# Centring of w_out ranked later on VectorE, and one more square of chunk 0 on ScalarE

## The chip, the cores and the metric

The kernel runs on one core of a Trainium2 chip. A core has five engines with instruction streams of their own: TensorE (PE) multiplies matrices, VectorE (DVE) and ScalarE (ACT) do elementwise work, GpSimd (POOL) does elementwise work on SBUF and issues the loads here, and SyncE (SP) issues stores and transposing transfers. All transfers run on the core's 16 DMA engines. The metric is the device time of one execution in microseconds (us); a profile's span is the part of it from the first to the last recorded instruction.

## What is computed

Linear attention without a mask, a norm over each head, and then an expert layer with a SoLU activation and a layer norm:

```python
# q, k, v: (8, 8, 576, 64); g_norm: (64,)
kv  = einsum('bhsd,bhse->bhde', k, v)
o   = einsum('bhsd,bhde->bhse', q, kv)
x   = o / sqrt(mean(o * o, -1) + 1e-6) * g_norm      # -> (4608, 512)
# w_in: (512, 1024); w_out: (1024, 512); g_ln: (1024,)
h   = x @ w_in
e   = exp(h - max(h)); u = h * e / sum(e)
ln  = (u - mean(u)) / sqrt(var(u) + 1e-6) * g_ln
out = ln @ w_out
```

The kernel does not divide by sum(e): it keeps u = h * exp(h) and takes the scale out of the layer norm at the end. For each token it needs the mean of u, of u squared and of e.

The subtraction of the mean is moved into the weights. w_out is multiplied by g_ln row by row, and the mean of the result over the 1024 rows is subtracted from each row. This is the centring. out is then u times the centred w_out, scaled by one number for each token.

## The kernel before

The tokens are worked through in nine chunks of 512: chunk c below 8 holds 512 of the 576 tokens of batch c, and chunk 8 holds the last 64 of every batch. A chunk goes through these pieces, which the source names as they are named here:

- `k`, `v`, `q`: loads on GpSimd (lines 212 and 220), for batches 0 and 1 in two halves. The buffers of each hold three batches.
- `kv_mm` (L286) and `kv` (L304, L306): the products of k and v, and their copies to SBUF, some of them on VectorE and some on ScalarE.
- `qT_mm` (L314) and `qT` (L321, L323): transposes of q on TensorE and their copies. From batch 4 on a transposing DMA on SyncE does this.
- `o_mm` (L348), `sq` (L363), `s_mm` (L369), `ln`, `ex` (L373, L377), `x` (L390): attention output, its square, the mean over a head, one over the root, and x.
- `h_mm` (L471), `exp` (L479), `u` (L486): eight blocks f = 0 to 7 of 128 columns of h, each 512 tokens wide.
- `usq` (L495 on ScalarE, L497 on GpSimd): the square of each block of u. `es` (L503, GpSimd): the sum of two neighbouring blocks of e.
- `sums` (L537): 80 narrow matmuls that sum u, usq and es over the columns. `turn` (L545) and `stats` (L553 to L558) on VectorE and `rstd` (L562, L564) on ScalarE make the scale of each token from them.
- `out` (L585): for each of four groups of 128 tokens two halves of four matmuls of u with the centred w_out. The first half uses blocks 0 to 3, the second blocks 4 to 7. `ob` (L617, VectorE) multiplies by the scale and `store` (L626, SyncE) writes 256 KB.

Once in the kernel, `w_mean` (L570) computes the mean over the rows of w_out into a PSUM bank, and eight pieces `w_center` (L576, VectorE) write the centred w_out in bf16, one for each block f. The first half of every `out` needs `w_center` 0 to 3, the second half 4 to 7.

The order on each engine is fixed when the program is built. Every piece is added to a plan with its engine, an assumed length, a rank, and the pieces that it needs. The planner then takes, again and again, the ready piece that can start first by its own reckoning, and the lower rank where several can start at the same time. PSUM banks and SBUF buffers enter through the fields `uses` and `first`: two banks each for h, out and o, one each for s and misc. The lists that come out are final: on the chip each engine works through its own and waits at each instruction for what it needs.

In chunk 0 the `usq` rank is fixed at -0.6 for all blocks, and `sums` has rank -0.4. Blocks 2, 4, 6 and 7 of `usq` are on ScalarE and the other four on GpSimd. The centring has ranks 0.05 to 0.89, and `u` of block 7 of chunk 0 has rank 0.875 + 0.04 = 0.915.

Of the kernel before, what the change touches and what calls it, by code (L numbers as in the profile page):

```python
# [84 lines left out]
def kernel(  # L85
# [27 lines left out]
    NC = B + 1  # L113
# [19 lines left out]
    plan = Plan({**banks, **bufs})  # L133
# [113 lines left out]
    for b in range(B):  # L247
        at = b - 9.0 if b > 1 else (-2.0, -1.5)[b]
        behind = [] if b < 2 else [("h_mm", 0, 0)] if b == 2 else ([("gate", b - 1)] if b - 1 in XBAR else []) + [("h_mm", b - 3, 2 if b == 3 else 0)]
        for g, hs in enumerate(heads(b)):  # L250
            part = 0.1 * g
            n = len(heads(b))
            for i, (name, src) in enumerate((("k", k), ("v", v))):
                plan.add((name, b, g), "pool", 0.75 if n == 1 else 0.6, at + part + 0.01 * i,
                         lambda name=name, src=src, b=b, hs=hs: load_kv(name, src, b, hs),
                         behind, uses=[(name, b)] if g else [],
# [3 lines left out]
                     uses=[("q", b)] if g else [], first=[] if g else [("q", b)], load=2.7 / n if b < 4 else 3.3)  # L260
# [11 lines left out]
    def kv_tag(b, x):  # L272
        return "s" if b > 1 and x else "misc"
# [123 lines left out]
    for c in range(NC):  # L397
# [4 lines left out]
        if c < B:  # L402
            for xs in ((0,), (1,)) if c < 2 else ((0, 1),):
# [3 lines left out]
                         uses=[("k", c), ("v", c)], first=[(kv_tag(c, x), "kv", c, x) for x in xs])  # L407
                for x in xs:
                    for part in range(3):
                        plan.add(("kv", c, x, part), kv_engine(c, x), 0.25, rg + 0.05,  # L410
                                 lambda c=c, x=x, part=part: kv_copy(c, x, part), [("kv_mm", c, g)],
                                 uses=[(kv_tag(c, x), "kv", c, x)])
        if c in XBAR:
            plan.add(("qT", c), "sp", 1.8, r - 0.1, lambda c=c: q_turn(c),
                     [("q", c, 0)] if c < B else [("q_last", b) for b in range(B)],
                     uses=[("q", c)] if c < B else [], first=[("qT", c)])
# [3 lines left out]
        for hf in range(2):  # L420
            g = group(c, hf)
            tag = ("out", "h")[c] if c < 2 and hf else "o"
            if c not in XBAR:
# [11 lines left out]
                     uses=[("qT", c)], first=[(tag, c, hf, z) for z in range(2)])  # L435
            for z in range(2):
                i = (c, hf, z)
                rz = r + w * (0.4 + 0.5 * hf + 0.12 * z)
                if (c, hf) in COPIED and z:
                    plan.add(("oc", i), "dve", 0.62, rz, lambda i=i: o_copy(*i), [("o_mm", c, hf)],  # L440
                             uses=[(tag, *i)], first=[("oc", i)])
                    plan.add(("sq", i), "pool", 1.05, rz + 0.01, lambda i=i: o_sq_copy(*i), [("oc", i)],
                             uses=[("oc", i)], first=[("osq", i)])
                else:
                    plan.add(("sq", i), "act", 0.57, rz, lambda i=i: o_sq(*i), [("o_mm", c, hf)],
                             uses=[(tag, *i)], first=[("osq", i)])
                stag = "h" if i in ((0, 0, 1), (0, 1, 0)) else "s"
                plan.add(("s_mm", i), "pe", 0.22, rz + 0.02, lambda i=i, stag=stag: s_mm(i, stag), [("sq", i)],
                         uses=[("osq", i)], first=[(stag, i)])
                if c == 0:  # L450
                    plan.add(("ex", i), "act", 0.6, rz + 0.04, lambda i=i: s_rsqrt(*i), [("s_mm", i)],
                             uses=[(stag, i)], first=[("rst", i)])
                else:
                    plan.add(("ln", i), "act", 0.6, rz + 0.03, lambda i=i: s_ln(*i), [("s_mm", i), "table"],
                             uses=[(stag, i)], first=[("lss", i)])
                    plan.add(("ex", i), "act", 0.6, rz + 0.04, lambda i=i: s_exp(*i), [("ln", i)],
                             uses=[("lss", i)], first=[("rst", i)])
                plan.add(("x", i), "dve", 0.67, rz + 0.06, lambda i=i: x_mul(*i),
                         [("ex", i)] + ([("x", (c, 0, 0))] if (hf, z) != (0, 0) else []),
                         uses=[(tag, *i), ("rst", i)] + ([("x", c)] if (hf, z) != (0, 0) else []),  # L460
# [3 lines left out]
    def h_bank(c, f):  # L464

        return ("h", "h", "o", "o", "out", "h", "h", "h")[f] if c == 0 else "h"

    def h_mm(c, f):
        t = T["h", c, f] = bank((h_bank(c, f),), [128, 512], FP32)
        for dt in range(NP):  # L470
            nc.tensor.matmul(  # L471
                t[:, :], w_in_sb[:, dt, f * 128:(f + 1) * 128], T["x", c][:, dt].rearrange("p a b c -> p (a b c)"),
                start=(dt == 0), stop=(dt == NP - 1),
            )

    def h_exp(c, f):
        if f % 2 == 0:
            T["e", c, f // 2] = tile_of(("e", c, f // 2), [128, 2, 512], FP32)
        nc.scalar.activation(  # L479
            out=T["e", c, f // 2][:, f % 2, :], in_=T["h", c, f][:, :], func=AF.Exp, bias=zero_t[:, :]  # L480
        )

    def h_u(c, f):
        if f == 0:
            T["u", c] = tile_of(("u", c), [128, NF, 512], BF16)
        nc.vector.tensor_tensor(  # L486
            out=T["u", c][:, f, :], in0=T["h", c, f][:, :], in1=T["e", c, f // 2][:, f % 2, :], op=MUL
        )

    def u_sq(c, f, engine):  # L490
        if f == 0:
            T["usq", c] = tile_of(("usq", c), [128, NF, 512], BF16)
        dst, src = T["usq", c][:, f, :], T["u", c][:, f, :]
        if engine == "act":
            nc.scalar.activation(out=dst, in_=src, func=AF.Square, bias=zero_t[:, :])  # L495
        else:
            nc.gpsimd.tensor_tensor(out=dst, in0=src, in1=src, op=MUL)  # L497

    def e_sum(c, n):
        if n == 0:  # L500
            T["es", c] = tile_of(("es", c), [128, NF // 2, 512], BF16)
        e = T["e", c, n]
        nc.gpsimd.tensor_tensor(out=T["es", c][:, n, :], in0=e[:, 0, :], in1=e[:, 1, :], op=ADD)  # L503

    xs = [(hf, z) for hf in range(2) for z in range(2)]
    for c in range(NC):
        for f in range(NF):
            r = c + f / 8
            plan.add(("h_mm", c, f), "pe", 0.87, r, lambda c=c, f=f: h_mm(c, f),
                     [("w_in", f // 4), *[("x", (c, *i)) for i in xs]], uses=[("x", c)], first=[(h_bank(c, f), "h", c, f)])  # L510
            plan.add(("exp", c, f), "act", 0.57, r + 0.02, lambda c=c, f=f: h_exp(c, f),
                     [("h_mm", c, f), "table"] + ([("exp", c, f - 1)] if f % 2 else []), uses=[(h_bank(c, f), "h", c, f)] + ([("e", c, f // 2)] if f % 2 else []),
                     first=[] if f % 2 else [("e", c, f // 2)])
            plan.add(("u", c, f), "dve", 0.62, r + 0.04, lambda c=c, f=f: h_u(c, f),
                     [("exp", c, f)] + ([("u", c, 0)] if f else []), uses=[(h_bank(c, f), "h", c, f), ("e", c, f // 2)] + ([("u", c)] if f else []),
                     first=[] if f else [("u", c)])
            engine = "act" if f in {0: (2, 4, 6, 7), 1: (), NC - 1: (1, 3, 5, 6, 7)}.get(c, (2, 6)) else "pool"
            plan.add(("usq", c, f), engine, 0.57 if engine == "act" else 1.05, r + 0.15 if c else -0.6,
                     lambda c=c, f=f, engine=engine: u_sq(c, f, engine), [("u", c, f)] + ([("usq", c, 0)] if f else []),
                     uses=[("u", c)] + ([("usq", c)] if f else []), first=[] if f else [("usq", c)])  # L520
            if f % 2:
                n = f // 2
                plan.add(("es", c, n), "pool", 1.28, r + 0.1, lambda c=c, n=n: e_sum(c, n),
                         [("exp", c, f)] + ([("es", c, 0)] if n else []), uses=[("e", c, n)] + ([("es", c)] if n else []),
                         first=[] if n else [("es", c)])
# [49 lines left out]
    def w_center(f):  # L575
        nc.vector.scalar_tensor_tensor(  # L576
            out=w_out_sb[:, f, :], in0=w_out_f[:, f, :].bitcast(FP32), scalar=g_ln_sb[:, f:f + 1],
            in1=T["mean"][:, :], op0=MUL, op1=SUB,
        )
# [48 lines left out]
    plan.add("w_mean", "pe", 2.0, -0.5, lambda: [w_mean(f) for f in range(NF)], ["w_out", "g_mean", ("o_mm", 0, 1)],  # L628
             first=[("out", "mean")])
    for f in range(NF):  # L630
        plan.add(("w_center", f), "dve", 0.67, 0.05 + 0.12 * f, lambda f=f: w_center(f), ["w_mean"], uses=[("out", "mean")])
    for c in range(NC):
        r, rs = (c + 1, c + 1) if c else (0.55, -0.5)
        parts = [[("u", c, f) for f in range(NF)], [("usq", c, f) for f in range(NF)], [("es", c, n) for n in range(NF // 2)]]
# [1 line left out]
                 uses=[("u", c), ("usq", c), ("es", c)], first=[("misc" if c else "h", "sum", c)])  # L636
        plan.add(("turn", c), "dve", 0.25, rs + 0.14, lambda c=c: sums_turn(c), [("sums", c)],
                 uses=[("misc" if c else "h", "sum", c)])
        plan.add(("stats", c), "dve", 0.65, rs + 0.16, lambda c=c: stats(c), [("turn", c)], uses=[("misc" if c else "h", "sum", c)])
        plan.add(("rstd", c), "act", 0.45, rs + 0.17, lambda c=c: rstd(c), [("stats", c)])  # L640
        for x in range(2 if c == NC - 1 else 0):
            engine = ("dve", "act")[x]
# [3 lines left out]
                     uses=[("h", "acc", x)] + ([("ob", c, 3)] if x else []), first=[] if x else [("ob", c, 3)])  # L646
            plan.add(("store", c, 3, x), ("sp", "act")[x], 0.6, r + 1.1, lambda x=x: store_cols(x), [("ob", c, 3, x)], uses=[("ob", c, 3)])
        for m in range(3 if c == NC - 1 else 4):
            tag = "o" if c == NC - 1 and m > 1 else "out"
            for half in range(2):  # L650
# [4 lines left out]
                         uses=[("u", c)] + ([(tag, c, m)] if half else []), first=[] if half else [(tag, c, m)])  # L655
# [37 lines left out]
```

## Time and profile before

| What | Value |
|---|---|
| Device time, median of 4 runs | 196.82 us (195.98 to 196.93) |
| Device time of the profiled execution | 196.84 us |
| Span of the profiled execution | 195.1 us |
| TensorE busy | 179.6 us, 92% of the span |
| VectorE busy | 122.6 us, 63% |
| ScalarE busy | 140.2 us, 72% |
| GpSimd busy | 129.3 us, 66% |
| Moved by the DMA queue of GpSimd's loads | 17.30 MB |
| The eight centrings, VectorE | 28.06 to 33.40 us |

The page gives the share of time in which each engine was busy, and the same for 40 equal slices of the span, one digit for each, in tenths. The chain of waits follows the work that ended last backwards, at each step to what released it. The timeline lists instructions in order of time: start, duration, engine, line, operation, output and inputs, with equal neighbours merged; in brackets stands how long the engine sat idle before it and what ended that idle time. A wait for several things is put down to the one that came last.

The centrings, with `u` of block 7 behind them, look like this on VectorE:

```profile
27.45 0.69 DVE L486 TENSOR_TENSOR u_sb<-h_ps,e_sb 128x512 bf16<-128x512 f32 x1 [0.77 <-ACT e_sb L479]
28.06 5.34 DVE L576 SCALAR_TENSOR_TENSOR w_out_sb<-w_out_f,g_ln_sb,out_ps 128x512 bf16<-128x512 f32 x8
33.32 0.68 DVE L486 TENSOR_TENSOR u_sb<-h_ps,e_sb 128x512 bf16<-128x512 f32 x1
```

### The profile page before, as it was taken

To read this page: it belongs to the slowest core of one execution; us is meant where nothing else is said; L and a number is where in the kernel's file an instruction comes from. 1 tells how busy PE (TensorE), PEld (TensorE's weight loads), DVE (VectorE), ACT (ScalarE), POOL (GpSimd) and SP (SyncE) were. 2 spreads that over 40 slices of the span, in tenths; PEclk is the share of its full clock that TensorE was granted. 3 is DMA by queue.
4 is the path that set the end of the run, shared out by engine and by line. 5 is a ranking of instruction groups with operands and counts; after the bars stand their busy time and mean duration, and the time that the engine had idled before them with its cause. 6 is when DMAs were issued, how large, how long until landed. Compare 5 with 4: busy or idle time off the path is not lost.

```text
span 195.1 us, 5441 instructions
## 1 busy us (share of the span) xinstructions
PE 179.6 (92%) x2282; PEld 88.6 (45%) x2282; DVE 122.6 (63%) x241; ACT 140.2 (72%) x244; POOL 129.3 (66%) x140
## 2 busy tenths in 40 slices
PE   7899896879689998999999999999999999999990
PEld 2343364544344443454445445445445554544560
DVE  1255679286866858648675965867594757666450
ACT  2027887979978897978879796988779496656420
POOL 7963599700689997796698977477385838846200
PEclk9999999999999999999999999999999999999999
DMA  3999999999994999999699995147111111211216
GB/s 49 171 202 266 356 203 205 203 207 271 229 200 65 165 203 223 174 180 197 162 171 217 209 197 142 59 91 192 57 54 57 57 54 57 108 57 54 109 21 197
DMA packets 36040, 29.71 MB, mean 152 GB/s; under 512 B 11816, under 2 KB 30512, under 8 KB 36016
## 3 DMA queue, kind: packets, MB, share of 16 engines
q0 software_dynamic: 20112, 17.30, 55.2%
q1 hardware_dynamic: 15616, 11.67, 20.7%
q10 hardware_dynamic: 288, 0.39, 0.6%
q8 instruction: 18, 0.29, 0.6%
q14 instruction: 6, 0.05, 0.1%
HBM read 32.51 MB, written 9.44 MB: 215 GB/s over the span
## 4 chain that ended last, share of the span: by engine, by line
PE 69%; DMA 15%; POOL 7%; ACT 3%; issue 2%; DVE 1%; POOLq 0%
PE out_ps L585 27%; PE h_ps L471 26%; DMA q_sb<-in_q_dram 11%; PE misc_ps L537 4%; DMA v_sb<-in_v_dram 4%; PE s_ps L369 3%; PE o_ps L348 3%; POOL usq_sb L497 2%; POOL k_sb L212 2%; POOL es_sb L503 1%; PE misc_ps L286 1%; PE misc_ps L193 1%; PE h_ps L595 1%; PE o_ps L585 1%; POOL v_sb L212 1%
## 5 line engine op out<-in xcount | busy, mean ns | idle before, releaser
L471 PE MATMUL h_ps<-x_sb,w_in_sb 128*128 128x512 bf16 x276 | 70.1, 379 | 1.1 <-DVE x_sb L390 1.1
L585 PE MATMUL out_ps<-w_out_sb,u_sb 128*128 128x512 bf16 x272 | 68.8, 379 | 2.2 <-DVE ob_sb L617 1.8
L497 POOL TENSOR_TENSOR usq_sb<-u_sb 128x512 bf16<-128x512 bf16 x51 | 52.9, 1045 | 22.1 <-DVE u_sb L486 21.8
L486 DVE TENSOR_TENSOR u_sb<-h_ps,e_sb 128x512 bf16<-128x512 f32 x69 | 47.3, 687 | 25.1 <-ACT e_sb L479 24.7
L503 POOL TENSOR_TENSOR es_sb<-e_sb 128x512 bf16<-128x512 f32 x36 | 45.8, 1272 | 23.6 <-ACT e_sb L479 23.4
L479 ACT ACTIVATE e_sb<-h_ps,zero_t 128x512 f32<-128x512 f32 x69 | 47.2, 683 | 13.4 <-PE h_ps L471 11.9
L471 PEld LDWEIGHTS <-w_in_sb 128*128 128x128 bf16 x288 | 27.2, 98 | 34.6 <-issue 4.0
L585 PEld LDWEIGHTS <-u_sb 128*128 128x128 bf16 x280 | 26.4, 98 | 33.8 <-issue 3.9
L390 DVE SCALAR_TENSOR_TENSOR x_sb<-o_ps,g_rep,rst_sb 128x512 bf16<-128x512 f32 x32 | 23.9, 750 | 11.0 <-ACT rst_sb L377 11.0
L617 DVE TENSOR_SCALAR ob_sb<-out_ps,rstd 128x512 f32<-128x512 f32 x33 | 24.5, 746 | 8.5 <-PE out_ps L585 4.4
L363 ACT ACTIVATE osq_sb<-o_ps,zero_t 128x512 bf16<-128x512 f32 x31 | 19.7, 682 | 13.9 <-PE o_ps L348 13.8
L373 ACT ACTIVATE lss_sb<-s_ps,eps_t 128x512 f32<-128x512 f32 x32 | 22.0, 688 | 3.0 <-PE s_ps L369 3.0
L377 ACT ACTIVATE rst_sb<-lss_sb,zero_t 128x512 f32<-128x512 f32 x32 | 23.3, 727 | 0.7
L495 ACT ACTIVATE usq_sb<-u_sb,zero_t 128x512 bf16<-128x512 bf16 x21 | 15.2, 722 | 6.1 <-DVE u_sb L486 6.0
L369 PE MATMUL s_ps<-osq_sb,head_mean 128*128 128x512 bf16 x34 | 12.9, 380 | 0.8 <-ACT lss_sb L373 0.4
L537 PEld LDWEIGHTS <-stat_sel 128*32 128x32 bf16 x720 | 10.1, 97 | 3.7 <-issue 3.2
L193 PE MATMUL s_ps<-zeros 128*128 128x512 bf16 x28 | 10.1, 488 | 1.4 <-DVE zero_t L158 1.2
L212 POOL DMA_DIRECT2D k_sb<-in_k_dram x10 | 7.8, 785 | 3.5 <-DMA w_in_sb<-in_moe_w_in_dram 2.0
L220 POOL DMA_DIRECT2D q_sb<-in_q_dram x10 | 8.6, 856 | 2.2 <-DMA w_in_sb<-in_moe_w_in_dram 1.5
L286 PE MATMUL misc_ps<-v_sb,k_sb 64*64 64x64 bf16 x360 | 7.6, 194 | 2.6 <-DMA v_sb<-in_v_dram 2.6
L286 PEld LDWEIGHTS <-k_sb 64*64 64x64 bf16 x576 | 6.8, 107 | 6.2 <-issue 6.2
L304 DVE CAST kvd<-misc_ps 64x128 bf16<-64x128 f32 (+1 forms) x24 | 6.9, 287 | 2.3 <-PE misc_ps L286 2.1
(86 smaller groups left out, 133.5 us busy)
## 6 DMA issues: line engine op xcount, KB each, us to landing
out_dram<-ob_sb SPq DMA_DIRECT2D x34, 256.0 KB, 3.4
k_sb<-in_k_dram POOLq DMA_DIRECT2D x6, 576.0 KB, 12.1
v_sb<-in_v_dram POOLq DMA_DIRECT2D x6, 576.0 KB, 12.4
q_sb<-in_q_dram POOLq DMA_DIRECT2D x6, 512.0 KB, 14.2
w_out_f<-in_moe_w_out_dram POOLq DMA_DIRECT2D x1, 2048.0 KB, 16.6
k_sb<-in_k_dram POOLq DMA_DIRECT2D x4, 288.0 KB, 11.9
v_sb<-in_v_dram POOLq DMA_DIRECT2D x4, 288.0 KB, 12.3
q_sb<-in_q_dram POOLq DMA_DIRECT2D x4, 256.0 KB, 12.2
```

The lines of the kernel that those rows point to most:

```text
L363: nc.scalar.activation(out=t[:, :], in_=T[("o", *i)].rearrange("p a b c -> p (a b c)"), func=AF.Square, bias=zero_t[:, :])
L369: nc.tensor.matmul(t[:, :], head_mean[:, :], T["osq", i][:, :], start=True, stop=True)
L373: nc.scalar.activation(out=t[:, :], in_=T["s", i][:, :], func=AF.Ln, bias=eps_t[:, :])
L377: nc.scalar.activation(out=t.rearrange("p a b c -> p (a b c)"), in_=T["lss", i][:, :], func=AF.Exp, scale=-0.5, bias=zero_t[:, :])
L390: nc.vector.scalar_tensor_tensor(out=T["x", c][:, 2 * hf:2 * hf + 2, z], in0=T["o", c, hf, z][:, :, :, :], scalar=g_rep[:, :], in1=T["rst" ...
L471: nc.tensor.matmul(t[:, :], w_in_sb[:, dt, f * 128:(f + 1) * 128], T["x", c][:, dt].rearrange("p a b c -> p (a b c)"), start=(dt == 0), st ...
L479: nc.scalar.activation(out=T["e", c, f // 2][:, f % 2, :], in_=T["h", c, f][:, :], func=AF.Exp, bias=zero_t[:, :])
L486: nc.vector.tensor_tensor(out=T["u", c][:, f, :], in0=T["h", c, f][:, :], in1=T["e", c, f // 2][:, f % 2, :], op=MUL)
L497: nc.gpsimd.tensor_tensor(out=dst, in0=src, in1=src, op=MUL)
L503: nc.gpsimd.tensor_tensor(out=T["es", c][:, n, :], in0=e[:, 0, :], in1=e[:, 1, :], op=ADD)
L585: nc.tensor.matmul(T["acc", c, m][:, :], T["u", c][:, f, m * 128:(m + 1) * 128], w_out_sb[:, f, :], start=(f == 0), stop=(f == NF - 1),)
L617: nc.vector.tensor_scalar_mul(out=t[:, :], in0=T["acc", c, m][:, :], scalar1=T["rstd", c][:, m:m + 1])
```

## The change

Two lines of the plan differ. The centring gets the ranks 0.8 to 1.08 in place of 0.05 to 0.89, and in chunk 0 the squares of blocks 1, 3, 5, 6 and 7 are made on ScalarE, those of blocks 0, 2 and 4 on GpSimd.

```diff
-            engine = "act" if f in {0: (2, 4, 6, 7), 1: (), NC - 1: (1, 3, 5, 6, 7)}.get(c, (2, 6)) else "pool"
+            engine = "act" if f in {0: (1, 3, 5, 6, 7), 1: (), NC - 1: (1, 3, 5, 6, 7)}.get(c, (2, 6)) else "pool"
...
     for f in range(NF):
-        plan.add(("w_center", f), "dve", 0.67, 0.05 + 0.12 * f, lambda f=f: w_center(f), ["w_mean"], uses=[("out", "mean")])
+        plan.add(("w_center", f), "dve", 0.67, 0.8 + 0.04 * f, lambda f=f: w_center(f), ["w_mean"], uses=[("out", "mean")])
```

What the planner makes of it, engine by engine, in the names of the pieces (chunk first, then block or group):

```
VectorE  before: w_center 0 1 2 3 4 5 6 7, u 0 7, x 1 0 0, turn 0, stats 0, x 1 0 1, ob 0 0, kv 2, ob 0 1
         after:  w_center 0 1 2, u 0 7, w_center 3 4 5 6 7, x 1 0 0, turn 0, stats 0, ob 0 0, x 1 0 1, ob 0 1, kv 2
ScalarE  before: exp 2 3, usq 2, exp 4 5, usq 4, exp 6, usq 6, exp 7, kv 1, qT 1 0, sq, sq, kv, usq 7, ...
         after:  exp 2, usq 1, exp 3 4 5, usq 3, exp 6, usq 5 6, exp 7, kv 1, usq 7, qT 1 0, sq, sq, kv, ...
GpSimd   before: usq 0, es 0, usq 1, load v2, usq 3, load q2, usq 5, load k3 v3, es 1, load q3, es 2 3, load k4 v4 q4
         after:  usq 0, es 0, usq 2, load v2, usq 4, load q2, es 1, load k3 v3, es 2, load q3, es 3, load k4 v4 q4
TensorE  before: out 0 1 0, s_mm, out 0 0 1, out 0 1 1, qT_mm 1 1, s_mm, sums 0, kv_mm 2, o_mm 1 1, out 0 2 0, out 0 2 1
         after:  s_mm, out 0 0 1, sums 0, qT_mm 1 1, s_mm, out 0 1 0, o_mm 1 1, out 0 1 1, kv_mm 2, out 0 2 0, out 0 3 0
```

Later in the lists three neighbourhoods are swapped. On TensorE the second block of h of chunk 1 and an `s_mm` of chunk 2 change places; in chunk 2 the block of h with f = 6 goes ahead of an `s_mm` of chunk 3. On VectorE `u` 2 4 goes ahead of `turn` 1 and `stats` 1, and `u` 2 6 ahead of an `x` of chunk 3. ScalarE takes `exp` 2 4, 2 5 and 2 6 each one place earlier. SyncE's list is the same.

## The prediction

> **What bounds the kernel now.** I read the page's parts 2 and 4 first, then the TensorE part of the timeline, then the DMA landings, then the other engines around the places where TensorE waits. The page first: the slices and the two rows of the chain.
>
> ```profile
> PE   7899896879689998999999999999999999999990
> DMA  3999999999994999999699995147111111211216
> GB/s 49 171 202 266 356 203 205 203 207 271 229 200 65 165 203 223 174 180 197 162 171 217 209 197 142 59 91 192 57 54 57 57 54 57 108 57 54 109 21 197
> ...
> PE 69%; DMA 15%; POOL 7%; ACT 3%; issue 2%; DVE 1%; POOLq 0%
> PE out_ps L585 27%; PE h_ps L471 26%; DMA q_sb<-in_q_dram 11%; PE misc_ps L537 4%; DMA v_sb<-in_v_dram 4%; PE s_ps L369 3%; PE o_ps L348 3%; POOL usq_sb L497 2%; POOL k_sb L212 2%; POOL es_sb L503 1%; PE misc_ps L286 1%; PE misc_ps L193 1%; PE h_ps L595 1%; PE o_ps L585 1%; POOL v_sb L212 1%
> ```
>
> A slice is 195.1 / 40 = 4.88 us. From slice 1 to slice 11, about 5 to 58 us, the DMA row is at 9 without a gap; the change lies inside that stretch. From about 54 us on TensorE is nearly full. The chain of waits shows where the two regimes meet:
>
> ```profile
> 30.94 0.88 POOL es_sb L503
> ...
> 32.16 22.13 DMA q_sb<-in_q_dram
> 54.30 0.05 issue
> 54.34 0.62 PE misc_ps L314 x8
> ```
>
> One q transfer of 512 KB takes 22.13 us from its issue. Issues of the same kind land in 12 to 14 us in the median, so most of this is waiting behind earlier transfers. On TensorE (start, duration, what; idle time before it and its releaser in brackets):
>
> ```profile
> 38.95 0.22 PE L286 MATMUL misc_ps<-v_sb,k_sb 64*64 64x64 bf16 x2 [0.64 <-DMA v_sb<-in_v_dram]
> 40.82 1.89 PE L585 MATMUL out_ps<-w_out_sb,u_sb 128*128 128x512 bf16 x8 [0.87 <-DVE ob_sb L617]
> 50.26 0.22 PE L286 MATMUL misc_ps<-v_sb,k_sb 64*64 64x64 bf16 x2 [1.05 <-DMA v_sb<-in_v_dram]
> 54.34 0.62 PE L314 MATMUL misc_ps<-ident,q_sb 128*128 128x128 bf16 x8 [1.14 <-DMA q_sb<-in_q_dram]
> 71.97 0.38 PE L369 MATMUL s_ps<-osq_sb,head_mean 128*128 128x512 bf16 x1 [0.41 <-ACT lss_sb L373]
> 74.17 2.75 PE L585 MATMUL out_ps<-w_out_sb,u_sb 128*128 128x512 bf16 x12 [0.96 <-DVE ob_sb L617]
> ```
>
> TensorE meets three transfers in its own order: v of batch 2 at 38.95, v of batch 3 at 50.26, q of batch 3 at 54.34. It waited for each of them. What it gains before 54.34 is given back there unless the transfers come earlier too.
>
> [...] landings of POOL's loads follow the order of issue (38.8, 41.4, 44.3, 50.1, 54.3 us for v2, q2, k3, v3, q3, each start plus its time to landing), and the two longest gaps are those in which the stores of chunk 0 run. [...] the trace's eight take 5.34 us, 0.667 each, which I use.
>
> **The change part by part, chunk 0 (24 to 54 us).** Seven of the eight centrings stay together in two groups; u of the last block moves from behind all eight to behind three. In the trace of before the eight start at 28.06. In the changed order three end at 28.06 + 3 x 0.667 = 30.06, u of block 7 takes 0.62 (start to start) to 30.7, and five more end at about 34.0 instead of 33.4. So u of block 7 is ready at 30.7 instead of 34.0 (3.3 us earlier), the fourth centring at 31.3 instead of 30.7, and the eighth 0.6 later.
>
> What waits for the centrings on TensorE: the first out matmuls of chunk 0 stood at 30.80 and now wait for the fourth centring, to about 31.3 (0.5 lost); the second half now waits for the eighth, 34.0 instead of 33.45 (0.55 later).
>
> The squares: ScalarE gets one more square of 0.57 to 0.72 us and takes 1, 3, 5, 6, 7; GpSimd loses one of 1.05 (four become three). ScalarE's fifth square stands where it waited 0.69 for TensorE before the copy of qT (31.00); that copy moves to about 31.3. GpSimd's own order puts a sum of e (1.28) where a square (1.05) stood ahead of the k, v and q issues of batch 3: these come 0.23 later (29.6, 30.4, 32.4), and the last sum of e ends at about 34.6 instead of 35.6, so the loads of batch 4 are issued 1 us earlier. No issue is moved past another; SP's list is the same.
>
> What this lets forward: the sums matmuls of chunk 0 need all u, squares and e sums. They stood at 37.01; now the last input is the e sum at 34.6, and they run at about 34.8 to 36.1. The statistics follow 1.4 later, rstd on ScalarE at about 38.2 behind the qT copy and one Ln, and the first scaled output ends at about 39.6 instead of 40.76. The out matmuls that waited for it (40.82, idle 0.87) start right behind the kv matmuls of batch 2, which still wait for v at 38.95: 38.95 + 0.6 = 39.6. That is 1.2 us ahead. A wait of about 0.5 for the second scaled output follows at 41.0, and the transposes of q2 meet a landing at 41.4 that is in time. I carry a lead of 1.0 us to the kv matmuls of batch 3.
>
> There the lead ends. TensorE reached them at 50.26 - 1.05 = 49.2; it now reaches them at 48.2 and waits 2.0 us for the same landing. Then kv, two blocks of h and o_mm (0.7 + 1.73 + 0.4) bring it to about 53.2 as before, and it waits 1.1 for q at 54.34. Gain at 54.34: nothing.
>
> **Why the landing doesn't move.** Before q3 stand the same loads in the same ring order and the same four stores of 256 KB, which in the trace are issued from 40.79 to 48.06 and so all begin before q3 has landed. At 29.6, when k3 is issued, v2 and q2 have still 9 to 12 us to go, so 0.23 us on the issue is covered by the backlog. If that cover were gone it would cost 0.25. Most of the stores come about 1 us earlier, which moves bytes between k3, v3 and q3; the sum ahead of q3 is the same. I take 0, with bounds of -0.8 and +0.5 as mixtures of reads and writes can share engines better or worse (205 GB/s without stores, 277 while they run in 44.4 to 48.8).
>
> **After 54.34.** TensorE's order is the same until 71.4, and it is full there: 16.58 busy of 16.60 from 54.4 to 71. Then one pair changes place: a block of h goes ahead of the s matmul that waited 0.41 for ScalarE. On VectorE u of chunk 2's block 4 goes ahead of turn and statistics of chunk 1. The rows of before:
>
> ```profile
> 70.42 0.33 DVE L545 STREAM_TRANSPOSE misc_ps<-misc_ps 128x128 f32<-128x128 f32 x1 [1.41 <-PE misc_ps L537]
> ...
> 71.21 0.17 DVE L558 TENSOR_REDUCE vare<-terms 128x4 f32<-128x12 f32 x1
> 71.37 0.69 DVE L486 TENSOR_TENSOR u_sb<-h_ps,e_sb 128x512 bf16<-128x512 f32 x1
> 72.70 0.75 DVE L390 SCALAR_TENSOR_TENSOR x_sb<-o_ps,g_rep,rst_sb 128x512 bf16<-128x512 f32 x1 [0.64 <-ACT rst_sb L377]
> 73.37 0.74 DVE L617 TENSOR_SCALAR ob_sb<-out_ps,rstd 128x512 f32<-128x512 f32 x1
> ```
>
> With exp now ahead of the square on ScalarE (70.04 instead of 70.67), u runs 70.8 to 71.4, turn starts at 71.4, and vare, 0.96 after the start of turn as before, is ready at 72.36. rstd starts on ScalarE at 72.58 in either order, since the same nine operations stand ahead of it from 67.93 on, two of them swapped. So 0.2 us of slack is left, the scaled output still starts at 73.37, and the out matmuls still wait for it to 74.17. The 0.41 is saved and the later wait becomes that much longer: 0 again. From 78 us on all orders are equal.
>
> **Sum.** Against the profiled execution: span 195.1, device time 196.84, so 1.74 lies outside. Change 0 + 0 + 0 gives a span of 195.1 and 196.8, which is also the median of the four (196.82).
>
> **Rivals.** (1) Faster: the landings move up. For it speaks that the chain names GpSimd's squares ahead of the q issue and that stores spread differently; against it the full DMA row and issues that come later, not earlier. At most TensorE's lead of 1.0 passes through: 196.8 - 1.0 = 195.8. (2) Slower at one place: turn and statistics of chunk 1, now behind u of block 4. It decides once that u ends later than 71.65; each further 0.1 goes to the out matmuls at 74.17. A start of exp held by 1.3 us gives 197.9. Against it: exp's input was written by 69.05. (3) Slower through q3: one store's share (256 KB at 205 GB/s, 1.3 us) falls ahead of it, 198.1; against it, all four stores already do. (4) The edit moves nothing that matters because VectorE is not late: excluded, since the sums do move up by 2 us; only their gain is lost.
>
> **Numbers.** No change: 0.80, with its own range 196.2 to 197.3 from the DMA bounds and the spread of the four runs. Faster rival 0.12, of which 0.11 beyond 0.5%; slower rivals 0.04 and 0.04, with 0.01 spill from the range of the first. Half a per cent, 0.98 us, is about what a measurement of this kernel can tell from no change. This gives 0.11, 0.80, 0.09. The range of 8 in 10 reaches to the faster rival: 195.7 to 197.5.
>
> **What would show it.** In the profile after: sums of chunk 0 at about 35 instead of 37; no wait of 0.87 for ob near 40; a wait near 2.0 for v at about 50.3 and one near 1.1 for q at about 54.3; the out matmuls of chunk 1 at about 74.2 with a longer wait. It is wrong if the q transposes start before 53.5 or after 55, or if the wait at 74.17 moves by more than 0.5.

## The result and the profile after

| | Before | Changed |
|---|---|---|
| Median | 196.25 us (56 runs, 195.58 to 196.97) | 196.39 us (35 runs, 195.25 to 197.87) |
| Profiled execution, device time | 196.84 us | 197.77 us |
| Its span | 195.1 us | 196.0 us |

The ratio is 1.0008, 95% interval 0.9995 to 1.0021: no change that can be told. But the spread is 2.6 us where it was 1.4. The mean TensorE clock of an execution splits the 36 changed ones that have it on record (the profiled one among them): 26 have 0.993 or more and a median of 196.07 us, 10 have 0.990 or less and a median of 197.51. The 56 runs of before have no clock on record. Of the 102 executions of the kernel before that were made beside the experiments below, 3 have 0.990 or less; they took 197.3 to 197.4 us.

The profile shown is of one of the 10. Its slices, by the page:

```profile
PE   7997988897699997999999999999999999999990
...
PEclk9999999999799999999999999999999999999998
DMA  3999999999994999899999973147111111211216
```

The DMA row is as full as before from slice 1 to slice 11. The clock row has a 7 in slice 10, near 50 us, which the row of before did not have.

The chain of waits now leads from the v of batch 3 (v3 from here on, and so for the others) into TensorE, where it was q3:

```profile
PE 71%; DMA 14%; POOL 7%; ACT 3%; issue 2%; DVE 1%; POOLq 0%
PE h_ps L471 27%; PE out_ps L585 27%; DMA v_sb<-in_v_dram 14%; PE misc_ps L537 4%; PE s_ps L369 3%; PE o_ps L348 3%; POOL usq_sb L497 2%; PE misc_ps L286 2%; POOL k_sb L212 2%; POOL es_sb L503 1%; PE misc_ps L193 1%; PE h_ps L595 1%; PE o_ps L585 1%; POOL v_sb L212 1%; ACT e_sb L479 1%
```

VectorE in the timeline, the place that was changed:

```profile
27.21 2.07 DVE L576 SCALAR_TENSOR_TENSOR w_out_sb<-w_out_f,g_ln_sb,out_ps 128x512 bf16<-128x512 f32 x3
29.20 0.68 DVE L486 TENSOR_TENSOR u_sb<-h_ps,e_sb 128x512 bf16<-128x512 f32 x1
29.80 3.37 DVE L576 SCALAR_TENSOR_TENSOR w_out_sb<-w_out_f,g_ln_sb,out_ps 128x512 bf16<-128x512 f32 x5
```

And TensorE at the places that were shown of before:

```profile
33.95 0.63 PE L537 MATMUL h_ps<-u_sb,stat_sel 128*32 128x128 bf16 x32
...
39.30 0.22 PE L286 MATMUL misc_ps<-v_sb,k_sb 64*64 64x64 bf16 x2 [0.85 <-DMA v_sb<-in_v_dram]
40.01 1.90 PE L585 MATMUL out_ps<-w_out_sb,u_sb 128*128 128x512 bf16 x8
...
50.84 0.22 PE L286 MATMUL misc_ps<-v_sb,k_sb 64*64 64x64 bf16 x2 [2.69 <-DMA v_sb<-in_v_dram]
51.89 3.12 PE L471 MATMUL h_ps<-x_sb,w_in_sb 128*128 128x512 bf16 x8
54.94 0.41 PE L348 MATMUL o_ps<-qT_sb,kvd 64*64 64x256 bf16 x8
55.29 0.62 PE L314 MATMUL misc_ps<-ident,q_sb 128*128 128x128 bf16 x8
...
75.11 2.75 PE L585 MATMUL out_ps<-w_out_sb,u_sb 128*128 128x512 bf16 x12 [1.42 <-DVE ob_sb L617]
```

The sums of chunk 0 start at 33.95 instead of 37.01, and the wait of 0.87 us for the scaled output near 40 us is gone. (In a second trace of the kernel before, of which lines are shown below, the sums start at 36.27 and this wait is 0.21.) TensorE then idles 2.69 us for v3, where it idled 1.05. The two blocks of h behind it take 3.12 us for eight matmuls. The second trace of the kernel before has 1.90 for the same eight. The windows view tells why (the columns are named in its first line, with the granted clock near the end):

```profile
core 0: us, PE busy (x) PEld busy (x) DVE busy (x) ACT busy (x) POOL busy (x), PEclk, DMA share, GB/s
48.00:51.00 3.00, 0.31 (x18) 0.19 (x21) 2.36 (x4) 1.96 (x4) 1.92 (x2) 1.00 1.29 246
51.00:54.40 3.40, 3.40 (x78) 1.71 (x70) 0.87 (x3) 1.31 (x4) 1.34 (x2) 0.50 1.21 228
54.40:57.00 2.60, 2.60 (x25) 1.29 (x24) 1.92 (x3) 2.12 (x5) 1.63 (x2) 1.00 1.23 205
```

After the idle time the clock is at 0.50 for 3.40 us, from 51.00 to 54.40, and at 1.00 behind it. The transposes of q3 no longer wait for q3, which landed at 53.47 here. They start at 55.29, behind the slow blocks. From there on the two take equally long: from the transposes to the end of the span it is 196.0 - 55.29 = 140.7 us, and 195.1 - 54.34 = 140.8 before.

### The profile page after: what moved, and what is told of

The parts are those of the page before. It is cut to its first block, busy times and chain, and to the rows that moved or that the text cites. A ratio compares the mean times of both kernels' runs of the same rounds, so it can differ in the third digit from the quotient of the medians.

```text
span 196.0 us, 5441 instructions
## 1 busy us (share of the span) xinstructions
PE 181.7 (93%) x2282; PEld 89.1 (45%) x2282; DVE 122.1 (62%) x241; ACT 140.3 (72%) x245; POOL 128.2 (65%) x139
## 4 chain that ended last, share of the span: by engine, by line
PE 71%; DMA 14%; POOL 7%; ACT 3%; issue 2%; DVE 1%; POOLq 0%
PE h_ps L471 27%; PE out_ps L585 27%; DMA v_sb<-in_v_dram 14%; PE misc_ps L537 4%; PE s_ps L369 3%; PE o_ps L348 3%; POOL usq_sb L497 2%; PE misc_ps L286 2%; POOL k_sb L212 2%; POOL es_sb L503 1%; PE misc_ps L193 1%; PE h_ps L595 1%; PE o_ps L585 1%; POOL v_sb L212 1%; ACT e_sb L479 1%
## 5 line engine op out<-in xcount | busy, mean ns | idle before, releaser
L471 PE MATMUL h_ps<-x_sb,w_in_sb 128*128 128x512 bf16 x276 | 71.4, 385 | 1.1 <-DVE x_sb L390 1.1
L497 POOL TENSOR_TENSOR usq_sb<-u_sb 128x512 bf16<-128x512 bf16 x50 | 51.8, 1046 | 22.8 <-DVE u_sb L486 22.7
L479 ACT ACTIVATE e_sb<-h_ps,zero_t 128x512 f32<-128x512 f32 x69 | 47.2, 684 | 13.9 <-PE h_ps L471 13.5
L495 ACT ACTIVATE usq_sb<-u_sb,zero_t 128x512 bf16<-128x512 bf16 x22 | 15.9, 721 | 4.9 <-DVE u_sb L486 4.7
```

The lines of the kernel that those rows point to most:

```text
L471: nc.tensor.matmul(t[:, :], w_in_sb[:, dt, f * 128:(f + 1) * 128], T["x", c][:, dt].rearrange("p a b c -> p (a b c)"), start=(dt == 0), st ...
L479: nc.scalar.activation(out=T["e", c, f // 2][:, f % 2, :], in_=T["h", c, f][:, :], func=AF.Exp, bias=zero_t[:, :])
```

## Experiments

Three theories. A: the landings of v3 and q3, behind full DMA engines, take TensorE's lead away. B: the longer idle time lets TensorE's clock fall in part of the executions, and these take longer, by the 1.4 us between the two medians above. Rival C: the lead would be lost in any case near 74 us, at the scaled output of chunk 1, where the change swaps work on VectorE. "Low clock" below means a mean clock of 0.990 or less in an execution. Ratios are to the kernel before, run on the same chip in the same session.

### Keep TensorE busy in the wait for v3

```diff
+    plan.add("warm3", "pe", 0.0, 0.0, lambda: warm(11, "misc"), [("h_mm", 1, 1)], first=[("misc", "warm3")])
...
-                plan.add(("kv_mm", c, g), "pe", 0.65, rg, lambda c=c, xs=xs: kv_mm(c, xs), [("k", c, g), ("v", c, g)],
+                plan.add(("kv_mm", c, g), "pe", 0.65, rg, lambda c=c, xs=xs: kv_mm(c, xs), [("k", c, g), ("v", c, g)] + (["warm3"] if c == 3 else []),
```

> The changed kernel with 11 extra matmuls of zeros (about 2.4 us) on TensorE between the second block of h of chunk 1 and the kv matmuls of batch 3, where it idled 2.69 us; they write a free PSUM bank and nothing reads them. Theory A (the landings of v3 and q3, behind a full DMA, take TensorE's lead away): the start of the kv matmuls stays at the landing. Theory B (the longer idle time also lets TensorE's clock fall to half for 3.4 us in part of the executions, which costs those about 1.3 us): with A, the clock stays at 0.995 or above in every run, no run is above 197.0, and the median is 195.7 to 196.1. If A holds and B does not: median 196.4 and runs up to 197.8 as in the changed kernel.

Measured: 196.07 us, ratio 1.0008 (0.9986 to 1.0029), low clock in 1 of 14 executions (198.17 us); the other 13 reach from 195.66 to 196.59. TensorE in the wait, and behind it:

```profile
47.39 2.54 PE L193 MATMUL misc_ps<-zeros 128*128 128x512 bf16 x11
50.69 1.90 PE L472 MATMUL h_ps<-x_sb,w_in_sb 128*128 128x512 bf16 x7
52.52 0.41 PE L349 MATMUL o_ps<-qT_sb,kvd 64*64 64x256 bf16 x8
52.86 0.62 PE L315 MATMUL misc_ps<-ident,q_sb 128*128 128x128 bf16 x8
```

The matmuls of zeros fill the wait, and the blocks of h take 1.90 us again (7 of the 8 are in the record). q3 landed at 52.75 and the transposes follow at 52.86. The median fits A and B together: it lies in the stated range and is still that of the kernel before. That the clock would stay at 0.995 or above in every execution was not met: it did in 11 of 14, and one of the others had the fall. 1 of 14 against 10 of 36 could also be chance; the next run has the larger contrast.

The same on the centring alone:

> The centring alone, with the 11 extra matmuls of zeros in TensorE's wait for v3. Theory B: the runs with a clock below 0.991, 8 of 14 for the centring alone, go to at most 1 of 14, and the median falls from 197.2 to 195.7 to 196.1. If the clock falls for another reason than the idle time there: the share of such runs stays near a half and the median near 197.

Measured: 196.46 us, ratio 1.0015 (0.9999 to 1.0031), no execution of 23 at 0.990 or less, two at 0.991 with 198.07 and 198.81 us. A stretch like the one above, 3.40 us at 0.50, takes 3.40 / 2 / 197 = 0.009 from the mean clock of a span of 197 us, an estimate, so a fall can also read 0.991. The trace is of one of these two. Behind the kv matmuls of batch 3 its blocks of h take 1.90 us; slow are the twelve matmuls of out at 74.44, with 4.44 us, where twelve of the changed kernel take 2.75 (at 75.11):

```profile
73.80 0.59 PE L472 MATMUL h_ps<-x_sb,w_in_sb 128*128 128x512 bf16 x2 [2.23 <-issue]
...
74.44 4.44 PE L586 MATMUL out_ps<-w_out_sb,u_sb 128*128 128x512 bf16 x12
```

Counted with these, 2 of 23 executions have a fall, where the centring alone, below, has 8 of 14. That is about what B said, and it shows that with the idle time in the wait for v3 filled most of the falls go. "issue" means that the engine waited for nothing that the profile shows. TensorE stops so ahead of matmuls of h in both traces with the matmuls of zeros (in the other for up to 1.6 us, between 70 and 90 us), where the traces of both kernels, of both with late or parked stores and of the fifth square alone have none of over 0.2 us between 70 and 80 us. The median came out 0.4 us above the stated range; whether these stops are why is open.

### One part of the change at a time

The centring alone (the ranks changed, the squares as before):

> Only the ranks of the centring changed; squares of chunk 0 as before. u of block 7 comes 3.3 us earlier, its square on ScalarE too, and GpSimd's list stays as before, so that the last sum of e still ends near 35 us and sums can start at about 35.5 instead of 37. Theory A: any lead is absorbed, 196.2 to 196.5. Theory B: if it reaches the wait for v3 as early as the changed kernel does, a part of the runs shows a clock below 0.992 and a time above 197; if it comes later, fewer do.

Measured: 197.20 us, ratio 1.0036 (1.0008 to 1.0064), low clock in 8 of 14. Those 8 have a median of 197.62, the other 6 of 195.82. A's range of 196.2 to 196.5 is missed, and the clock makes the difference. TensorE waits 2.85 us for v3, as in the whole change (2.69, 2.52 and 2.95 in its three traces), and the blocks of h are slow behind it (the line has 6 of the 8 matmuls):

```profile
50.62 0.22 PE L286 MATMUL misc_ps<-v_sb,k_sb 64*64 64x64 bf16 x2 [2.85 <-DMA v_sb<-in_v_dram]
52.17 2.69 PE L471 MATMUL h_ps<-x_sb,w_in_sb 128*128 128x512 bf16 x6 [0.22 <-issue]
```

The fifth square alone (the centring as before):

```diff
-            engine = "act" if f in {0: (2, 4, 6, 7), 1: (), NC - 1: (1, 3, 5, 6, 7)}.get(c, (2, 6)) else "pool"
+            engine = "act" if f in {0: (1, 3, 5, 6, 7), 1: (), NC - 1: (1, 3, 5, 6, 7)}.get(c, (2, 6)) else "pool"
```

> Only the fifth square on ScalarE; centring as before, so u of block 7 stays behind all eight centrings and its square stands at 34 us or later. Theory A: sums start near 35 to 35.5, TensorE arrives at the wait for v3 up to 1 us earlier than before, and all of it is absorbed: 196.0 to 196.3. Theory B: its wait for v3 is shorter than that of the centring alone (2.85 us), so at most 2 of 14 runs show a clock below 0.991 and a time above 197.

Measured: 195.58 us, ratio 0.9970 (0.9957 to 0.9984), low clock in 1 of 22. Its waits:

```profile
49.27 0.22 PE L286 MATMUL misc_ps<-v_sb,k_sb 64*64 64x64 bf16 x2 [1.58 <-DMA v_sb<-in_v_dram]
53.05 0.62 PE L314 MATMUL misc_ps<-ident,q_sb 128*128 128x128 bf16 x8 [0.84 <-DMA q_sb<-in_q_dram]
```

The low clocks are as few as B said. A was too strict: I expected 196.0 to 196.3, and the part alone is faster than the kernel before by 0.6 us. It still waits for both landings, but q3 landed 14.6 us after v2, against 14.9 and 15.5 us in the two traces of before. The last store of chunk 0 was issued at 46.2 here and at 46.9 and 47.7 there. That an earlier store is what frees q3 fits these numbers, but is only argued. Adding a part also makes the planner reorder the lists around it, so that the two parts are not independent.

### Take the stores out of the way of the loads

The four stores of chunk 0 go behind the first transposing transfer on SyncE. This is the only list that differs.

```diff
-                     [("ob", c, m)], uses=[("ob", c, m)])
+                     [("ob", c, m)] + ([] if c else [("qT", 4)]), uses=[("ob", c, m)])
```

On the changed kernel:

> The changed kernel with the four stores of chunk 0 issued behind the transposing transfer of q of batch 4 on SyncE; all other lists equal. Theory A: 1 MB at about 205 GB/s is 5 us less ahead of q3, and 3 to 4 us less ahead of v3, so v3 lands near 47.5 and q3 near 50, the waits of 2.7 us there go, and the time falls by 2.5 to 3.2 us against the kernel before, to 193.0 to 193.8. Rival C (the lead is lost in any case at the scaled output of chunk 1, near 74 us): the wait there grows by what is gained earlier, and the time is within 0.5 us of the changed kernel.

On the kernel before:

> The kernel before with the same late stores of chunk 0. Theory A: its waits for v3 and q3 (1.05 and 1.14 us) go, 1.8 to 2.2 us, to 194.0 to 194.5; so the changed kernel with late stores is faster than this one by about 1.0 us, which is the lead that the change makes on TensorE and that the landings hid. Rival C: both the same, within 0.5 us of the kernel before.

Measured: 195.61 us (0.9973, 0.9959 to 0.9987) and 195.42 us (0.9973, 0.9952 to 0.9994). The landings did what A said: v3 at 47.29 and 46.93, q3 at 50.00 and 49.65. So did TensorE, as far as chunk 1: its out matmuls started at 71.50 and 72.23 instead of 75.11 and 74.17. But the times missed the range by 1 to 2 us, and the two kernels came out alike, as rival C had said. The traces put the loss at another place than C: the stores, now at 60 us, delay q5. It was issued at 62.48 and was there at 78.75, after 16.3 us; in the changed kernel with the stores at their old place it took 11.3 (65.67 to 76.95). On GpSimd of the changed kernel with late stores:

```profile
78.75 0.18 POOL L335 COPY landed<-q_sb 1x1 bf16<-1x1 bf16 x1 [4.56 <-DMA q_sb<-in_q_dram]
```

and on TensorE from 78 to 120 us, total, times and longest wait:

```profile
PE misc_ps L537 <- POOL usq_sb L497: 1.2, 2, 0.8
```

A copy of one element on GpSimd stands until q5 has landed, the squares stand behind it, and the sums of chunks 2 and 3 wait for the squares. The lead is taken once more by a landing, two batches later. To see what the change is worth without that, the stores have to leave the loads altogether. So chunk 0 gets four output buffers of its own, and its stores go behind the last transposing transfer, near 129 us, when the last load has landed:

```diff
-        "ob": 4,
+        "ob": 4, "ob0": 4,
...
-        t = T["ob", c, m] = tile_of(("ob", c, m), [128, d_model], FP32)
+        t = T["ob", c, m] = tile_of(("ob" if c else "ob0", c, m), [128, d_model], FP32)
...
-                     [("out", c, m, 1), ("rstd", c)], uses=[(tag, c, m)], first=[("ob", c, m)])
+                     [("out", c, m, 1), ("rstd", c)], uses=[(tag, c, m)], first=[("ob" if c else "ob0", c, m)])
...
-                     [("ob", c, m)], uses=[("ob", c, m)])
+                     [("ob", c, m)] + ([] if c else [("qT", 8)]), uses=[("ob" if c else "ob0", c, m)])
```

On the changed kernel, the kernel before, and the fifth square alone:

> The changed kernel with the four stores of chunk 0 kept in four output buffers of their own and issued behind the last transposing transfer, near 130 us, where the DMA engines are mostly idle; all other lists equal. Theory A: no load up to q of batch 7 shares the engines with these stores, so the waits for v3 and q3 go, and GpSimd's wait of 4.56 us for q5 with the less late stores goes too. The out matmuls of chunk 1 start near 71.5 us and nothing takes this back: 193.2 to 194.0 us. Rival C: within 0.5 us of the kernel with the less late stores, 195.6.

> The kernel before with the same parked stores. Theory A: waits of 2.2 us go, one of 0.6 for ScalarE comes (as with the less late stores), so the out matmuls of chunk 1 start near 72.2 us: 194.0 to 194.6, that is 0.5 to 0.9 us above the changed kernel with parked stores, the part of the change's lead that is left when no landing takes it. Rival C: no difference between the two, and both near 195.5.

> The fifth square on ScalarE with the centring as before, and the stores of chunk 0 parked as in the two kernels with parked stores. Theory A: its lead on TensorE ahead of the landings was about 1.1 us against 1.4 for the whole change, so it lies 0.2 to 0.5 us above the changed kernel with parked stores (193.96): 194.1 to 194.5. If the centring is what makes the lead, it lies near the kernel before with parked stores, 195.0.

| Stores parked | Median | Ratio (95% interval) | Out matmuls of chunk 1 start |
|---|---|---|---|
| Changed kernel | 193.96 us | 0.9887 (0.9865 to 0.9908) | 71.63 us |
| Fifth square alone | 194.31 us | 0.9899 (0.9878 to 0.9920) | 71.73 us |
| Kernel before | 195.05 us | 0.9941 (0.9918 to 0.9963) | 72.33 us |

TensorE of the changed kernel with parked stores:

```profile
48.77 0.22 PE L286 MATMUL s_ps<-v_sb,k_sb 64*64 64x64 bf16 x2 [0.52 <-ACT lss_sb L373]
...
71.63 2.75 PE L585 MATMUL out_ps<-w_out_sb,u_sb 128*128 128x512 bf16 x12 [1.42 <-DVE ob_sb L617]
```

and of the kernel before with parked stores:

```profile
49.46 0.22 PE L286 MATMUL s_ps<-v_sb,k_sb 64*64 64x64 bf16 x2 [0.63 <-ACT lss_sb L373]
...
70.13 0.38 PE L369 MATMUL s_ps<-osq_sb,head_mean 128*128 128x512 bf16 x1 [0.41 <-ACT lss_sb L373]
72.33 2.75 PE L585 MATMUL out_ps<-w_out_sb,u_sb 128*128 128x512 bf16 x12 [0.96 <-DVE ob_sb L617]
```

No wait for a load of batch 3 is left here, ScalarE's Ln is what the kv matmuls wait for, and the lead of 49.46 - 48.77 = 0.69 us is still 0.70 at the out matmuls and 0.7 at the end (spans 192.5 and 193.2). By the medians the change is now worth 1.1 us; the two traces account for 0.7 of it. The kernel before with parked stores is 0.45 us above its stated range, and why is open; the other two lie in theirs. That shows A: with the landings out of the way the lead reaches the end. It also refutes C: the wait near 72 us is longer by about what the wait of 0.41 was, as the two traces show, and takes nothing of the lead. The kernel with both the change and the parked stores is the best of the study, 1.1% faster than the kernel before.

### Second and third profiles

> The kernel before, a second look. In the profiles so far the end of the span is 140.7 to 141.1 us after the transposes of q3 start, and these start at the later of q3's landing and v3's landing plus 2.9 us of TensorE work. Theory A: the same holds here, the transposes follow q3 at once, with TensorE idle 0.5 to 1.3 us before them; the landing of q3 itself moves by up to 1 us from one execution to the next, about as the device time does (195.5 to 197.1).

```profile
36.27 0.63 PE L537 MATMUL h_ps<-u_sb,stat_sel 128*32 128x128 bf16 x32
...
40.07 1.89 PE L585 MATMUL out_ps<-w_out_sb,u_sb 128*128 128x512 bf16 x8 [0.21 <-DVE ob_sb L617]
...
49.34 0.22 PE L286 MATMUL misc_ps<-v_sb,k_sb 64*64 64x64 bf16 x2 [0.95 <-DMA v_sb<-in_v_dram]
50.05 1.90 PE L471 MATMUL h_ps<-x_sb,w_in_sb 128*128 128x512 bf16 x8
51.88 0.41 PE L348 MATMUL o_ps<-qT_sb,kvd 64*64 64x256 bf16 x8
53.66 0.62 PE L314 MATMUL misc_ps<-ident,q_sb 128*128 128x128 bf16 x8 [1.37 <-DMA q_sb<-in_q_dram]
```

The second trace of before has 196.16 us and a span of 194.4. The transposes start 0.68 us earlier than in the first, at 53.66, right after q3 landed at 53.61 (the idle time of 1.37 is just above the 1.3 expected), and the end is 0.7 earlier. In these two, the difference in time is the difference of this landing; that the whole spread of the kernel before comes from it is likely, and not shown by two traces.

> The changed kernel, a second look. Theory A and B: with the clock at 0.993 or more the wait for v3 is 2.3 us or more, the two blocks of h behind it take about 1.9 us instead of 3.1, the transposes start at v3's landing plus 2.9, and the time is 195.3 to 196.7. With the clock at 0.990 or less: 3.1 us again and 197.2 to 197.9. A wait for v3 under 2 us with a low clock would speak against B.

> The changed kernel, a third look, to catch an execution without the fall of the clock. [...] Theory B: if the clock stays up, the idle time before the kv matmuls of batch 3 is again near 2.5 us [...]; the transposes start at v3's landing plus 2.9 and the time is 195.3 to 196.7. [...]

Both executions of the changed kernel had the low clock: 197.39 and 197.76 us, waits for v3 of 2.52 and 2.95 us, and the blocks of h at 3.23 and 3.31 us. So there is no trace of the changed kernel with its clock up; what was expected of such an execution was not tested, and how long it waits for v3 stays open.

## Why the prediction was right, and where it was not

The likeliest case was no change at 196.8 us in a range of 195.7 to 197.5; the median is 196.39. The kernel before has a median of 196.25 over 56 runs, so the execution that the sum was made against, 196.84, was one of its longer ones.

- *What the change brings forward.* Right. The sums were put at 34.8 us and start at 33.95, in an execution in which the first centring also started 0.85 earlier. The arrival at the kv matmuls of batch 3 was put at 48.2; it is 50.84 - 2.69 = 48.15. This is nearer than the working deserves: 1.2 us ahead less a wait of 0.5 leaves 0.7, and the text carries 1.0; the wait near 41.0 did not come, and v2 landed 0.35 later than in the sum. From v2's landing to the arrival it is 8.98 us in all three traces of the changed kernel, and 10.40 and 9.67 in the two of before. So the lead is 1.4 or 0.7 us, and 0.7 is also what the parked stores show. (The text says that seven of the eight centrings stay together. All eight do, three and five, and its sum counts them so.)
- *The landings take it.* Right, and shown by the parked stores. But the sum held both landings fixed, and both moved. Counted from v2's landing, v3 came after 11.4 to 11.8 us in the three traces, against 10.5 and 11.3 in the two of before, and q3 after 13.9 to 14.4, against 14.9 and 15.5. The wait for v3, put at 2.0 us, is 2.69, 2.52 and 2.95. The text did say that earlier stores move bytes between k3, v3 and q3; it gave this no price at v3, and at q3 took 0 inside bounds of -0.8 and +0.5. That the two shifts go opposite ways is luck.
- *What the longer wait does.* Missed. A wait of over 2 us was taken as lost time and nothing else. In the traces with a wait for v3 of 2.52, 2.69 and 2.95 us, two blocks of h behind it take 3.23, 3.12 and 3.31 us instead of 1.90; in the one of 2.69 the clock there is 0.50. By the prediction's own test, a start of the transposes after 55 us, this step was wrong: they started at 55.29. The cause was not q3, which landed at 53.47. The slower cases in the list were about VectorE and about q3; none was about TensorE's clock.
- *The swap near 71 us.* Right. The 0.41 wait went and the later wait grew from 0.96 to 1.42.
- *Why the sum is still near zero.* The falls of the clock, 10 of 36 executions times 1.4 us, cost 0.4 us in the mean, and the median hides most of it. With the clock up the median is 196.07, 0.2 below the 56 runs of before. The means are 196.46 and 196.30. A small gain and a cost that the prediction did not have cancel, and that is luck too.
- *The two parts.* The prediction treated them as one. The runs part them: the fifth square alone is worth 0.6 us, so "nothing" was wrong for it, and the centring alone costs 0.7 by its ratio, through the clock. Even with the clock up the whole change (196.07) lies 0.5 above the square alone (195.54 in 21 executions of another session). A reason that fits, and was not tested: in the changed kernel the first two stores are issued at 38.94 and 40.26, ahead of 39.60 and 41.85 with the square alone, and k3 lands at 46.89 instead of 44.30. With the stores parked the square is worth 0.74 us by the medians. The centring adds 0.35 to it, but the two medians are from different sessions, their ratios overlap, and the traces show 0.10 (71.73 and 71.63): this is not clear of the noise.

## What to carry to other kernels

Work brought forward in front of a transfer is worth, as far as these runs show, only what the transfer itself comes earlier: with the stores out of the way the change is worth 1.1 us by the medians, with them in place nothing that can be told. What shares the DMA engines with that transfer, here four stores that no engine was waiting for, is the thing to move, and far enough that the next load is not the one that pays. A lead that only lengthens one idle stretch of TensorE can even cost time, as it did here through the clock (the centring alone: 197.62 us in the 8 executions with the low clock, 195.82 in the other 6); compare the mean clock of every execution when a spread widens.

## What was not expected of the hardware

That a wait of TensorE of this length is followed by a lower clock was not in the prediction. In the profile of the changed kernel TensorE idles 2.69 us ahead of 50.84, and the granted clock is 1.00 from 48.00 to 51.00, 0.50 to 54.40 and 1.00 to 57.00. All traces in which TensorE waits for v3, by the length of the wait:

| Trace | Wait for v3 | Matmuls of the two blocks of h behind it | Mean clock of the execution |
|---|---|---|---|
| Kernel before, second | 0.95 us | eight in 1.90 us | 1.000 |
| Kernel before | 1.05 us | eight in 1.90 us | 0.998 |
| Fifth square alone | 1.58 us | eight in 1.90 us | 1.000 |
| Changed kernel, second | 2.52 us | eight in 3.23 us | 0.990 |
| Changed kernel | 2.69 us | eight in 3.12 us | 0.987 |
| Centring alone | 2.85 us | six in 2.69 us | 0.988 |
| Changed kernel, third | 2.95 us | eight in 3.31 us | 0.988 |

Two stops of TensorE at another place go with these. The one of 2.23 us in the centring with the matmuls of zeros has the slow matmuls of out behind it, 4.44 us instead of 2.75, in an execution with a mean clock of 0.991. The one of 1.6 us in the changed kernel with the matmuls of zeros is in an execution with a mean clock of 0.996.

So the stretches of 2.23 us and more had slow matmuls behind them, and the waits for v3 of up to 1.58 us did not. That is what was measured in nine executions, and no limit for another kernel follows from it. Why only a part of the executions has the fall was not shown: 26 of the 36 of the changed kernel have a mean clock of 0.993 or more, and no trace is of one of them.
